# Words and stores of a float64 weight preparation moved to ScalarE, with a clamp conversion, earlier word loads and a fifth weight buffer

## The chip, the cores and the metric

One core of one Trainium2 chip. The metric is device time of the whole program in microseconds (us), the median of the runs. One run of each kernel was recorded by the profiler. Its times by stage are from that single run. The groups of experiments ran on four chips (3, 4, 5 and 14); each ratio is to the kernel before, run in the same rounds on the same chip.

## The reference

```python
# attention, per head: softmax of q over its 64 features, softmax of k over the 576 positions
q_s = exp(q - q.max(-1));  q_s = q_s / (q_s.sum(-1) + 1e-9)
k_s = exp(k - k.max(2));   k_s = k_s / (k_s.sum(2) + 1e-9)
kv  = einsum('bhsd,bhse->bhde', k_s, v)
x   = einsum('bhsd,bhde->bhse', q_s, kv)            # then heads side by side: (8, 576, 512)
# Fourier mixing, layer norm, two layers
u   = x + real(fft(fft(x, axis=1), axis=2))
un  = (u - mean(u)) / sqrt(var(u) + 1e-6)
out = u + maximum(un @ w_ch1, 0) @ w_ch2            # 512 -> 2048 -> 512; w_ch1, w_ch2 come as float64
```

## The kernel before

The two layers run as a Strassen-like scheme of 7 products. For each layer the weights are cut into 8 pairs of chunks. Each pair comes from DRAM as pairs of 32-bit words (float64), is converted, gets four additions for the seven combinations, and is stored to DRAM, from where the later batches load it. Batch 0 uses the first layer's pairs as they are prepared. The work of one batch on TensorE (PE), "up" (first layer) and "down" (second layer), is interleaved with the attention and Fourier work ("front") of the next batch.

```python
def wtile(self):                                           # the ring of weight buffers
    return self.work.tile([P, NP, HD], F32, tag="w", name="w", bufs=4)

def convert(self, place, t):                               # float64 words -> float32
    ...                                                    # lo, hi: low and high words; ti: t as int32
    nc.scalar.activation(lo, lo.bitcast(U32), ACT.Copy, scale=2.0 ** -29)
    V.tensor_scalar(out=ti, in0=hi, scalar1=3, scalar2=0x3FFFFFFF, op0=ALU.logical_shift_left, op1=ALU.bitwise_and)
    V.scalar_tensor_tensor(out=ti, in0=hi, scalar=-(1 << 30), in1=ti, op0=ALU.bitwise_and, op1=ALU.bitwise_or)
    least = float(np.array(0x38100000, np.uint32).view(np.float32))
    nc.scalar.activation(hi.bitcast(F32), hi.bitcast(F32), ACT.Abs)
    V.scalar_tensor_tensor(out=t, in0=hi.bitcast(F32), scalar=least, in1=t, op0=ALU.is_ge, op1=ALU.mult)
    nc.gpsimd.tensor_tensor(out=ti, in0=ti, in1=lo, op=ALU.add)

def prepare(self, layer, p, places):
    w = self.wtile()
    for i in range(2):
        self.convert(places[i], w[:, 2 * i:2 * i + 2, :].rearrange("p a n -> p (a n)"))
    (self.b_side if layer else self.a_side)(lambda i: w[:, i, :], nc.gpsimd, nc.vector)   # 4 additions
    if layer == 0:
        nc.sync.dma_start(self.w1s[p][:], w[:, 0:7, :]);  self.stream[p] = w
    else:
        nc.sync.dma_start(self.w2s[:, :, p, :].rearrange("s p n -> p s n"), w[:, 0:7, :])

def used(self, n):                                         # PE is done with weight tile n
    self.stream.pop(n)
    if n >= NP:
        self.load(n + 4)                                   # loads run four tiles ahead

def q_load(self, it):
    q = self.work.tile([P, D], F32, tag="q", name="q", bufs=3)
    ...
# main loop
for g in range(B + 1):
    jobs, down = blk.up(g, unT, h), blk.down(g, h)
    side = front(g + 1) ...
    cut = len(side) * 2 // 3                               # this part beside up, the rest beside down
    merged(start(blk, jobs, h) if g == 0 else flat(jobs), side[:cut])
    merged(down, side[cut:] + norm(g + 1))
```

## Time and profile before

| | before |
|---|---|
| time | 1390.59 us (1386.94 to 1391.18) |
| first product of the first layer, batch 0 | 110.2 us |
| first product of the second layer, batch 0 | 289.8 us |
| end of batch 1's first layer | 398.6 us |
| from there to the last matmul | 960.1 us |

The marks are start times of PE's instructions in the timeline. Up to the second mark PE often waits. The prediction shows the lines that this rests on.

### The profile page before, as it was taken

How to read it: one execution, taken by the hardware profiler on the slowest of the kernel's cores; microseconds unless marked ns; L12 is line 12 of the kernel's file. 1: busy time of each engine (PE TensorE's matmuls, PEld its weight loads, DVE VectorE, ACT ScalarE, POOL GpSimd, SP SyncE). 2: the span in 40 equal slices, each digit the busy share in tenths (PEclk: the TensorE clock that was granted, in tenths of full speed). 3: DMA queues.
4: the chain of work that ended last, by engine and by line, in shares of the span. 5: the costliest groups of instructions: out<-in, count | busy, mean ns of one | idle time of the engine just before them, and what ended most of it. 6: DMA issues, size and time to landing. Idle time of an engine off the chain costs nothing.

```text
span 1384.5 us, 14661 instructions
## 1 busy us (share of the span) xinstructions
PE 1226.2 (89%) x5676; PEld 1003.1 (72%) x5676; DVE 580.0 (42%) x1146; ACT 326.7 (24%) x590; POOL 422.1 (30%) x350
## 2 busy tenths in 40 slices
PE   4578677399899998999999999999999999999992
PEld 3437563288787876788778877887788778788882
DVE  3948876821513254335713542364234242502200
ACT  2624342410310142114301421142014101201200
POOL 1624566710530125003600450045013401321310
PEclk7558785589999999999999999999999999999996
DMA  5922334575342543156424542454253335455421
GB/s 170 306 68 69 137 128 163 190 265 164 141 152 88 172 159 146 67 167 198 158 98 138 193 159 77 145 197 152 88 146 130 150 103 174 150 178 179 165 102 45
DMA packets 90279, 203.46 MB, mean 147 GB/s; under 512 B 22241, under 2 KB 56033, under 8 KB 82145
## 3 DMA queue, kind: packets, MB, share of 16 engines
q1 hardware_dynamic: 90208, 202.52, 43.2%
q8 instruction: 45, 0.74, 0.2%
q14 instruction: 26, 0.20, 0.0%
HBM read 177.33 MB, written 29.88 MB: 150 GB/s over the span
## 4 chain that ended last, share of the span: by engine, by line
PE 74%; DVE 10%; POOL 6%; DMA 4%; issue 2%; ACT 1%; SPq 0%; POOLq 0%; DVEq 0%; ACTq 0%
PE bb L590 14%; PE bb L555 11%; PE bc L590 9%; PE ba L590 9%; PE ba L555 7%; PE bc L555 6%; PE acc L402 5%; DMA q<-in_q_dram 3%; PE acc L289 3%; PE acc L427 2%; POOL w L192 1%; PE acc L424 1%; PE tr L486 1%; PE acc L405 1%; POOL eo L384 1%
## 5 line engine op out<-in xcount | busy, mean ns | idle before, releaser
L555 PE MATMUL bb<-unT,w 128*128 128x256 f32 x864 | 218.8, 395 | 46.6 <-DVE u L525 39.6
L555 PEld LDWEIGHTS bb<-unT,w 128*128 128x128 f32 x864 | 166.5, 197 | 78.3 <-DVE u L525 46.3
L590 PE MATMUL bb<-w,h 128*128 128x256 f32 x864 | 198.5, 381 | 0.0
L590 PEld LDWEIGHTS bb<-w,h 128*128 128x128 f32 x864 | 161.5, 190 | 28.4 <-issue 7.3
L555 PE MATMUL ba<-unT,w 128*128 128x256 f32 x576 | 142.5, 387 | 0.0
L196 POOL TENSOR_TENSOR h<-h 128x512 f32<-128x512 f32 x36 | 46.1, 1279 | 313.4 <-ACT h L567 313.4
L555 PE MATMUL bc<-unT,w 128*128 128x256 f32 x576 | 140.5, 381 | 0.0
L590 PE MATMUL bc<-w,h 128*128 128x256 f32 x576 | 131.4, 381 | 0.0
L590 PE MATMUL ba<-w,h 128*128 128x256 f32 x576 | 128.0, 379 | 0.0
L590 PEld LDWEIGHTS bc<-w,h 128*128 128x128 f32 x576 | 107.5, 190 | 18.0 <-issue 4.4
L555 PEld LDWEIGHTS ba<-unT,w 128*128 128x128 f32 x576 | 109.2, 194 | 15.7 <-issue 1.0
L590 PEld LDWEIGHTS ba<-w,h 128*128 128x128 f32 x576 | 109.2, 190 | 15.4 <-issue 0.8
L555 PEld LDWEIGHTS bc<-unT,w 128*128 128x128 f32 x576 | 107.0, 190 | 15.3 <-DVE h L566 0.9
L567 ACT ACTIVATE h<-h 128x512 f32<-128x512 f32 x108 | 68.1, 631 | 190.8 <-DVE h L566 190.5
L604 POOL TENSOR_TENSOR x<-x,u 128x512 f32<-128x512 f32 x18 | 23.3, 1293 | 254.4 <-DVE u L528 172.2
L402 PE MATMUL acc<-ft,eo 128*128 128x289 f32 (+3 forms) x240 | 83.3, 472 | 7.5 <-POOL eo L386 7.4
L402 PEld LDWEIGHTS acc<-ft,eo 128*128 128x128 f32 (+3 forms) x240 | 39.6, 183 | 42.3 <-issue 26.0
L525 DVE TENSOR_TENSOR u<-bb,s 128x512 f32<-128x512 f32 x45 | 31.0, 689 | 89.1 <-PE bb L555 54.3
L318 POOL TENSOR_TENSOR q<-q,qm 128x512 f32<-128x512 f32 x36 | 41.8, 1170 | 82.2 <-DVE qm L317 33.1
L528 DVE TENSOR_TENSOR u<-bb,s 128x512 f32<-128x512 f32 x45 | 31.0, 689 | 77.5 <-PE bb L555 45.4
L289 PE MATMUL acc<-v,ks 128*128 128x128 f32 (+1 forms) x320 | 55.5, 317 | 6.1 <-ACT ks L277 4.1
L566 DVE TENSOR_TENSOR h<-bc,u 128x512 f32<-128x512 f32 x72 | 49.6, 689 | 24.0 <-PE bc L555 23.0
(134 smaller groups left out, 1540.0 us busy)
## 6 DMA issues: line engine op xcount, KB each, us to landing
w<-w2s SPq DMA_DIRECT2D x63, 1024.0 KB
w<-w1s SPq DMA_DIRECT2D x64, 896.0 KB
k<-in_kT_dram SPq DMA_DIRECT2D x32, 288.0 KB
h<-in_w_dram SPq DMA_DIRECT2D x18, 512.0 KB
v<-in_v_dram SPq DMA_DIRECT2D x32, 256.0 KB
q<-in_q_dram SPq DMA_DIRECT2D x32, 256.0 KB
w1s<-w SPq DMA_DIRECT2D x8, 896.0 KB
w2s<-w SPq DMA_DIRECT2D x8, 896.0 KB
```

The costliest lines, as they stand in the source:

```text
L196: e1.tensor_tensor(out=at(4), in0=at(2), in1=at(3), op=ALU.add)
L289: nc.tensor.matmul(pk, lhsT=ks[0:n, c, :], rhs=v[0:n, c, :], start=(c == 0), stop=(c == NC - 1))
L318: nc.gpsimd.tensor_tensor(out=heads, in0=heads, in1=spread(m), op=ALU.subtract)
L402: nc.tensor.matmul(pz, lhsT=eo[c][int(odds)][s, cols], rhs=self.ft[s, 3 * int(odds) + c, :], start=(c == 0), stop=(c == 2 and odds))
L427: nc.tensor.matmul(pb, lhsT=z(2 + k), rhs=self.cd[:, 2 + k, 0:HD - 1], start=(k == 0), stop=(k == 1))
L525: V.tensor_tensor(out=temp("u2"), in0=box["bb"][:], in1=box["s1"][:], op=ALU.add)
L528: V.tensor_tensor(out=temp("u3"), in0=box["bb"][:], in1=box["s1"][:], op=ALU.add)
L555: nc.tensor.matmul(bank()[:, i, :], lhsT=w[:, A_AT[m], k * P:(k + 1) * P], rhs=unT[:, B_AT[m], k, :], start=first and i == 0 and k == 0, s ...
L566: V.tensor_tensor(out=at(i), in0=bank[:], in1=u[:], op=ALU.add)
L567: nc.scalar.activation(at(i), at(i), ACT.Relu)
L590: nc.tensor.matmul(bank()[:, i, :], lhsT=h[:, p, A_AT[m], i * P:(i + 1) * P], rhs=w[:, p, :], start=first and i == 0 and p == 0, stop=p == ...
L604: nc.gpsimd.tensor_tensor(out=x, in0=x, in1=t[:], op=ALU.add)
```

## The change

The intent: the start waits on SyncE's one queue and on VectorE (DVE), whose instructions take longer beside GpSimd's (in the trace before the 32 of L185 take 0.42 us on average where no GpSimd instruction runs beside them, 16 times, and 0.91 us, up to 1.52, where one does). So words and stores go to ScalarE's (ACT's) queue, the first layer's words are asked for during batch 0's attention, all combinations go to DVE, the conversion gets a cheaper clamp, batch 0's queries get buffers of their own, and a fifth buffer lets a fifth pair be ready early. The diff, cut to its core:

```diff
-        return self.work.tile([P, NP, HD], F32, tag="w", name="w", bufs=4)
+        return self.work.tile([P, NP, HD], F32, tag="w", name="w", bufs=5)
 def words(...)
-            self.nc.sync.dma_start(place..., w1[...])
+        dma = self.nc.scalar.dma_start
 def convert(...)
+        least = float(np.array(0x38000000, np.uint32).view(np.float32))
+        nc.scalar.activation(t, hi.bitcast(F32), ACT.Abs)
+        V.tensor_scalar_max(t, t, least)
+        V.tensor_scalar(out=ti, in0=ti, scalar1=3, scalar2=0x3FFFFFFF, op0=ALU.logical_shift_left, op1=ALU.bitwise_and)
         V.scalar_tensor_tensor(out=ti, in0=hi, scalar=-(1 << 30), in1=ti, op0=ALU.bitwise_and, op1=ALU.bitwise_or)
-        V.scalar_tensor_tensor(out=t, in0=hi.bitcast(F32), scalar=least, in1=t, op0=ALU.is_ge, op1=ALU.mult)
 def prepare(...)
-        (self.b_side if layer else self.a_side)(lambda i: w[:, i, :], nc.gpsimd, nc.vector)
+        (self.b_side if layer else self.a_side)(lambda i: w[:, i, :], self.nc.vector, self.nc.vector)
+    def send(self, layer, p, w):                       # called one pair later
+        self.nc.scalar.dma_start(to, w[:, 0:7, :])
+    def follow(self, t):                               # called after each exp of batch 0's keys and queries
+        if self.first:
+            place, run = self.first.pop(0)
+            self.nc.scalar.copy(place[0:1, 0:1], t[0:1, 0:1])
+            run()                                      # issues one pair of first-layer words
 def q_load(...)
+        if b == 0:
+            q = self.halves()[:, 0:D]                  # six other buffers, not the three of "q"
 def t_load(...): three fewer loads of the shared first query
-            steps.insert(2, blk.tables)
+            steps.insert(4, blk.tables)
-        cut = len(side) * 2 // 3
+        cut = len(side) * (1 if g == 0 else 2) // 3
+            weights.early()                            # before batch 0's front
+            merged(weights.first(jobs), [])
+            merged(weights.second(), side[:cut])
```

More of the change, by code (lines that the diff above doesn't have):

```diff
@@ L137, in __init__ @@
         self.cd = c.tile([P, 5, NN], F32, name="cd")
-        self.xs, self.live, self.stream = {}, {}, {}
+        self.xs, self.live, self.stream, self.first = {}, {}, {}, []
         self.turns = 0
@@ L164, in wtile, with words, convert @@
     def wtile(self):
-        return self.work.tile([P, NP, HD], F32, tag="w", name="w", bufs=4)
-    def words(self, layer, f, place):
+        return self.work.tile([P, NP, HD], F32, tag="w", name="w", bufs=5)
+    def words(self, layer, p, place):
+        dma = self.nc.scalar.dma_start
         if layer == 0:
-            w1 = self.w1.bitcast(I32).rearrange("(k p) n -> p k n", p=P)
-            self.nc.sync.dma_start(place.bitcast(I32).rearrange("p (k n) -> p k n", k=KT),
-                                   w1[:, :, f * 2 * P:(f + 1) * 2 * P])
-        else:
-            w2 = self.w2.bitcast(I32).rearrange("(f p) n -> p f n", p=P)
-            self.nc.sync.dma_start(place.bitcast(I32), w2[:, f, :])
-    def convert(self, place, t):
+            w1 = self.w1.bitcast(I32).rearrange("(k p) (i f n) -> i p k f n", p=P, i=2, f=NP)
+            for i in range(2):
+                dma(place[:, i * 2 * D:(i + 1) * 2 * D].bitcast(I32).rearrange("p (k n) -> p k n", k=KT),
+                    w1[i, :, :, p, :])
+        else:
+            w2 = self.w2.bitcast(I32).rearrange("(i f p) n -> p i f n", p=P, i=2)
+            dma(place.bitcast(I32).rearrange("p (i n) -> p i n", i=2), w2[:, :, p, :])
+    def convert(self, place, t, adder):
         nc, V = self.nc, self.nc.vector
@@ L181, in convert @@
         ti = t.bitcast(I32)
-        nc.scalar.activation(lo, lo.bitcast(U32), ACT.Copy, scale=2.0 ** -29)
-        V.tensor_scalar(out=ti, in0=hi, scalar1=3, scalar2=0x3FFFFFFF, op0=ALU.logical_shift_left,
+        least = float(np.array(0x38000000, np.uint32).view(np.float32))
+        nc.scalar.activation(t, hi.bitcast(F32), ACT.Abs)
+        V.tensor_scalar_max(t, t, least)
+        V.tensor_scalar(out=ti, in0=ti, scalar1=3, scalar2=0x3FFFFFFF, op0=ALU.logical_shift_left,
                         op1=ALU.bitwise_and)
         V.scalar_tensor_tensor(out=ti, in0=hi, scalar=-(1 << 30), in1=ti, op0=ALU.bitwise_and, op1=ALU.bitwise_or)
-        least = float(np.array(0x38100000, np.uint32).view(np.float32))
-        nc.scalar.activation(hi.bitcast(F32), hi.bitcast(F32), ACT.Abs)
-        V.scalar_tensor_tensor(out=t, in0=hi.bitcast(F32), scalar=least, in1=t, op0=ALU.is_ge, op1=ALU.mult)
-        nc.gpsimd.tensor_tensor(out=ti, in0=ti, in1=lo, op=ALU.add)
+        nc.scalar.activation(lo, lo.bitcast(U32), ACT.Copy, scale=2.0 ** -29)
+        adder.tensor_tensor(out=ti, in0=ti, in1=lo, op=ALU.add)
     def a_side(self, at, e1, e2):
@@ L206, in b_side, with prepare @@
         e1.tensor_tensor(out=at(6), in0=at(2), in1=at(5), op=ALU.subtract)
-    def prepare(self, layer, p, places):
-        nc = self.nc
+    def prepare(self, layer, p, place):
         w = self.wtile()
         for i in range(2):
-            self.convert(places[i], w[:, 2 * i:2 * i + 2, :].rearrange("p a n -> p (a n)"))
-        (self.b_side if layer else self.a_side)(lambda i: w[:, i, :], nc.gpsimd, nc.vector)
+            self.convert(place[:, i * 2 * D:(i + 1) * 2 * D],
+                         w[:, 2 * i:2 * i + 2, :].rearrange("p a n -> p (a n)"), self.nc.gpsimd)
+        (self.b_side if layer else self.a_side)(lambda i: w[:, i, :], self.nc.vector, self.nc.vector)
         if layer == 0:
-            nc.sync.dma_start(self.w1s[p][:], w[:, 0:7, :])
             self.stream[p] = w
-        else:
-            nc.sync.dma_start(self.w2s[:, :, p, :].rearrange("s p n -> p s n"), w[:, 0:7, :])
+        return w
+    def send(self, layer, p, w):
+        to = self.w2s[:, :, p, :].rearrange("s p n -> p s n") if layer else self.w1s[p][:]
+        self.nc.scalar.dma_start(to, w[:, 0:7, :])
     def load(self, n):
@@ L268, in k_exp @@
         self.live[it].append(rec)
+        self.follow(k)
+    def follow(self, t):
[3 more added lines that the diff above has]
+            run()
     def k_turn(self, it):
@@ L296, in q_load @@
         _, b, c, u = it
-        q = self.work.tile([P, D], F32, tag="q", name="q", bufs=3)
+        if b == 0:
+            q = self.halves()[:, 0:D]
+        else:
+            q = self.work.tile([P, D], F32, tag="q", name="q", bufs=3)[:]
         for part, tok in tokens(c, u):
@@ L303, in t_load @@
         _, b, u = it
-        q = self.work.tile([P, D], F32, tag="q", name="q", bufs=3)
+        q = self.work.tile([P, D], F32, tag="q", name="q", bufs=3)[:]
+        dma = self.nc.sync.dma_start
+        if not u:
+            dma(q[0::Q], self.q[b:b + 4, 0, :])
         for j in range(4):
-            for part, tok in tokens(2, u):
-                part = slice(Q * j + part.start, Q * j + part.stop)
-                self.nc.sync.dma_start(q[part], self.q[b + j, tok, :])
+            part, tok = tokens(2, u)[-1]
+            dma(q[Q * j + part.start:Q * j + part.stop], self.q[b + j, tok, :])
         self.live[it] = [q]
@@ L313, in q_exp @@
         q = self.live[it][0]
-        heads = q[:].rearrange("p (h d) -> p h d", h=H)
+        heads = q.rearrange("p (h d) -> p h d", h=H)
         spread = lambda t: t[:].unsqueeze(2).to_broadcast([P, H, DH])
@@ L318, in q_exp @@
         nc.gpsimd.tensor_tensor(out=heads, in0=heads, in1=spread(m), op=ALU.subtract)
-        nc.scalar.activation(q[:], q[:], ACT.Exp)
+        nc.scalar.activation(q, q, ACT.Exp)
+        self.follow(q)
         rec = self.small.tile([P, H], F32, tag="qrec", name="qrec", bufs=3)
@@ L677, in flat @@
         return [s for step in steps for s in step]
-    for step in front(0):
-        step()
-    for step in norm(0):
-        step()
     for g in range(B + 1):
+        h = hpool.tile([P, NP, 7, HD], F32, tag="h", name="h")
+        if g == 0:
+            weights = Weights(blk, h)
+            weights.early()
+            merged(front(0) + norm(0), [])
         unT = nexts.pop(g)
-        h = hpool.tile([P, NP, 7, HD], F32, tag="h", name="h")
         jobs, down = blk.up(g, unT, h), blk.down(g, h)
@@ L690 @@
             side = blk.reload() if g + 1 == B else []
-        cut = len(side) * 2 // 3
+        cut = len(side) * (1 if g == 0 else 2) // 3
         if g == 0:
-            first = start(blk, jobs, h)
-            merged(first, side[:cut])
+            merged(weights.first(jobs), [])
+            merged(weights.second(), side[:cut])
         else:
@@ L698 @@
         merged(down, side[cut:] + (norm(g + 1) if g < B else []))
-def start(blk, jobs, h):
-    at = h[:].rearrange("p a s n -> p (a s n)")
-    inside = lambda r: at[:, r * 2 * D:(r + 1) * 2 * D]
-    places = {}
-    def fetch(layer, p, where):
-        places[layer, p] = where
-        for i in range(2):
-            blk.words(layer, p + i * NP, where[i])
-    def prepare(layer, p):
-        blk.prepare(layer, p, places.pop((layer, p)))
-    def fetch_in(layer, p, r):
-        return lambda: fetch(layer, p, [inside(r), inside(r + 1)])
-    def fetch_out(p, spare):
-        def run():
-            if spare:
-                t = blk.work.tile([P, 7, 2, HD], F32, tag="unT", name="words", bufs=1)[:].rearrange(
-                    "p a k n -> p (a k n)")
-            else:
-                t = blk.wtile()[:].rearrange("p a n -> p (a n)")
-            fetch(1, p, [t[:, i * 2 * D:(i + 1) * 2 * D] for i in range(2)])
-        return run
-    def ready(layer, p):
-        return lambda: prepare(layer, p)
-    steps = [fetch_in(0, p, 2 * p) for p in range(3)] + [fetch_in(0, p, 2 * p - 2) for p in range(4, NP)]
-    steps += [ready(0, 0), fetch_in(0, 3, 0)] + [ready(0, p) for p in range(1, 4)]
-    steps += jobs[0] + [ready(0, 4), ready(0, 5)] + jobs[1] + [ready(0, 6), ready(0, 7), fetch_in(1, 0, 12)]
-    steps += jobs[2] + [ready(1, 0), fetch_out(1, False), ready(1, 1)] + jobs[3]
-    for p in range(2, NP):
-        steps += [fetch_out(p, p % 2 == 0), ready(1, p)]
-    return steps + [lambda i=i: blk.load(NP + i) for i in range(4)]
@@ new lines, with __init__, fetch, ready @@
+class Weights:
+    def __init__(self, blk, h):
+        self.blk, self.h, self.places, self.last = blk, h[:].rearrange("p a s n -> p (a s n)"), {}, None
+    def fetch(self, layer, p, at):
+        def run():
+            place = self.h[:, at * 4 * D:(at + 1) * 4 * D] if isinstance(at, int) else at()[:, 0:4 * D]
+            self.blk.words(layer, p, place)
+            self.places[layer, p] = place
+        return run
+    def ready(self, layer, p):
+        def run():
+            w = self.blk.prepare(layer, p, self.places.pop((layer, p)))
+            self.send()
+            self.last = (layer, p, w)
+        return run
+    def send(self):
+        if self.last is not None:
+            self.blk.send(*self.last)
+        self.last = None
+    def early(self):
+        for p in (0, 1, 2, 4, 5, 6, 7):
+            at = p if p < 3 else p - 1
+            self.blk.first.append((self.h[:, at * 4 * D:(at + 1) * 4 * D], self.fetch(0, p, at)))
+    def first(self, jobs):
+        ready, fetch = self.ready, self.fetch
+        steps = [ready(0, 0), fetch(0, 3, 0)] + [ready(0, p) for p in range(1, 5)]
+        steps += jobs[0] + [ready(0, 5), ready(0, 6)]
+        steps += jobs[1] + [ready(0, 7), fetch(1, 0, 6), ready(1, 0)]
+        return steps + jobs[2] + [fetch(1, 1, self.ring), ready(1, 1)] + jobs[3]
+    def second(self):
+        steps = []
+        for p in range(2, NP):
+            steps += [self.fetch(1, p, self.ring if p % 2 else self.spare), self.ready(1, p)]
+        return steps + [self.send] + [lambda i=i: self.blk.load(NP + i) for i in range(4)]
+    def ring(self):
+        return self.blk.wtile()[:].rearrange("p a n -> p (a n)")
+    def spare(self):
+        return self.blk.work.tile([P, 7, 2, HD], F32, tag="unT", name="words", bufs=1)[:].rearrange("p a k n -> p (a k n)")
```

## The prediction

> **What bounds the kernel now.** I read the page first, then the busy times by stretch, then the DVE and GpSimd groups of the first 290 us, then who waited for whom in that stretch, for the queue of SyncE (SP) too. In the slices of the page PE is full from about 290 us on, and before that its clock falls to half again and again:
>
> ```profile
> PE   4578677399899998999999999999999999999992
> DVE  3948876821513254335713542364234242502200
> PEclk7558785589999999999999999999999999999996
> ```
>
> The stretches are cut at three marks of PE's timeline: 110 us (batch 0's attention, Fourier step and norm are done, the first product of the first layer starts), 204 us (the first layer of batch 0 is done), 290 us (the first product of the second layer starts). The columns are span, busy us of each engine with instruction counts, granted clock, DMA share, GB/s.
>
> ```profile
> 0.00:110.00 110.00, 61.91 (x203) 40.18 (x204) 66.13 (x143) 40.91 (x75) 39.01 (x45) 0.62 0.55 179
> 110.00:204.00 94.00, 70.14 (x341) 59.99 (x340) 77.31 (x126) 34.23 (x63) 52.27 (x43) 0.86 0.32 108
> 204.00:290.00 86.00, 52.81 (x161) 33.83 (x160) 59.30 (x113) 29.97 (x53) 50.61 (x42) 0.54 0.62 204
> 290.00:1384.50 1094.50, 1041.38 (x4977) 869.05 (x4975) 377.24 (x765) 221.60 (x401) 280.21 (x221) 0.98 0.42 143
> ```
>
> After 290 us PE is busy 1041 of 1094 us at clock 0.98, and some 26 us of what is missing is the closing tail: nothing in the change can take much there. Before 290 us PE does 185 us of work, much of it at half clock; busy times clock is 61.91 x 0.62 + 70.14 x 0.86 + 52.81 x 0.54 = 127 us, so 163 us of the start are lost. The start is where float64 weights, held as pairs of words, become float32: 8 pairs of chunks of each layer, each with two conversions, additions for the seven combinations, and a store. The second layer's product cannot start before the last of these stores has landed. So the path is: batch 0's front, conversions, first layer (its weights are kept in 4 buffers, so pairs 4 to 7 wait until PE has used pairs 0 to 3), conversions of the second layer, store, load.
>
> In this path DVE is the engine nearest to full (77.3 of 94 us, then 59.3 of 86), and much of its time isn't its own. The GpSimd row belongs to the same work (columns: busy us, mean ns):
>
> ```profile
> L191 DVE SCALAR_TENSOR_TENSOR w<-h,w 128x512 f32<-128x512 f32 x18 | 22.1, 1232 | 1.2 <-ACT h L190 1.1
> L187 DVE SCALAR_TENSOR_TENSOR w<-h,w 128x512 int32<-128x512 int32 x18 | 16.4, 914 | 0.0
> L185 DVE TENSOR_SCALAR w<-h 128x512 int32<-128x512 int32 x18 | 13.0, 735 | 0.2 <-PE bc L555 0.2
> L192 POOL TENSOR_TENSOR w<-w,h 128x512 int32<-128x512 int32 x18 | 25.9, 1444 | 26.9 <-DVE w L191 23.7 <-DVE qrec L322 2.5 <-issue 0.7
> ```
>
> The reader is to compare these means with the undisturbed durations of the same instructions, which the view of a single line gives: 0.68, 0.68, 0.42 and 1.27 us. The loss is 0.55 + 0.23 + 0.32 = 1.1 us of DVE per conversion.
>
> The second thing is order. SP issues everything, in one queue, and a store whose data isn't ready stops the loads behind it. These are SP's waits from 20 to 110 us (total, times, longest):
>
> ```profile
> SPq L216 <- DVE w L199: 39.8, 3, 24.3
> SPq L251 <- PE tr L279: 17.4, 1, 17.4
> SPq L299 <- DVE q L324: 8.7, 2, 6.3
> ```
>
> L216 is the store of combinations. In SP's timeline it stands waiting from 78 to 103 us, and only at 120.7 us is the next load of batch 1's keys issued. L299 is a load of queries that waits for one of three buffers: batch 0's query loads go out at 22.9, 33.9 and 39.5 us, and the first words of weights only at 25.4 us, though the DMA engines moved only 20 to 90 GB/s from 18 to 24 us and reach over 330 when fed.
>
> [...]L185 takes 0.42 us alone and up to 1.52 us[...]. [...]here 1.27 against 0.69 us for 128x512, so 1.84, and 0.72 against 0.42 for the 128x256 of the combinations. [...]
>
> **The change part by part.**
>
> Conversion. The clamp takes the place of the comparison and product: one tensor_scalar maximum (taken as L185's 0.42 us, same shape and kind) for the 0.685 us of L191. DVE per conversion: 0.42 + 0.42 + 0.685 = 1.53 us instead of 1.79. ACT stays at two instructions of 0.67 us.
>
> Combinations. All four additions of a pair go to DVE: 1.68 us instead of 0.84 (layer one) or 0.42 (layer two). DVE per pair, undisturbed: 2 x 1.53 + 1.68 = 4.7 us, against 4.4 and 4.0 before. GpSimd per pair: 2 x 1.27 = 2.5 us, against 4.0 and 4.7 undisturbed.
>
> Sum of both. Undisturbed DVE rises by 8 x 0.3 + 8 x 0.7 = 8 us. As run before, the conversions and combinations took DVE some 100 us (layer one 16 x 2.88 + 11.0 = 57, layer two 37.2 + 5.5 = 43), of which 33 us are over the undisturbed times. GpSimd's share in this work falls from some 83 us to about 43, so I halve the 33: DVE becomes 16 x 4.7 + 17 = 92. Only 7 us come from here; but the hops DVE to GpSimd to DVE within a pair go (POOL waited 44.8 us for L191 in all, DVE 12.7 us in the second and third stretches for GpSimd's parts of a pair).
>
> Early words. Seven of eight pairs of the first layer (1 MB each) are issued from ScalarE as keys and queries have been exponentiated, from about 6 us on, and batch 0's queries get buffers of their own. To land in the first stretch: 8.4 MB of words, 3.5 of attention inputs, 0.5 of shared queries, 1.65 of tables, 14 MB; at some 340 GB/s that is 41 us, against about 65 before. DVE sits idle for some 23 us before 35 us and 19 between 69 and 104; five pairs (the fifth buffer) fit there. The first stretch is bounded by the queries' chain, then by the Fourier step at half clock (48 us from 62 to 110, unchanged). The last queries come about 13 us earlier: 110 becomes 97.
>
> First layer. Five pairs are ready instead of four, only three are left (3 x 5.7 = 17 us of DVE with contention, instead of 28), and batch 1's attention isn't merged in as main work but fills gaps. PE needs 4 x 14 us for the four jobs; at 18 us each with the waits, 72 instead of 94: minus 22.
>
> Second layer. Six pairs at 5.7 us are 34 us, the rest of batch 1's front and norm some 20 us on DVE: 54 against 59 before, so nothing from work. Fetches no longer stand behind SP's stores (55 us of SP's waits from 110 to 290 are at the second layer's stores): 86 becomes 78.
>
> After that. Less of batch 2's front is done ahead (some 10 us of PE time at full clock lie in 266 to 290 now), partly given back by the fifth weight buffer, which lets SP issue loads without waiting for PE: plus 4.
>
> Cost on ScalarE: 16 + 8 loads of words and 16 stores, 40 issues of about 0.4 us (SP's durations) and seven tiny copies of 0.19 us, 17 us in 290, where it is busy 105; beside other work unless a send waits. Three fewer query loads per shared block save 1.5 us of SP, hidden.
>
> Sum: -13 - 22 - 8 + 4 = -39 us; 1390.6 - 39 = 1352.
>
> **The rivals.** (a) ScalarE becomes the blocked queue: a store or fetch in its order waits, and the evictions behind it stop PE. For: SP waited up to 24 us on one store. Against: each store is put one pair later, when its data should be done. It would give back 20 to 30 us: 1375 to 1385. (b) DVE is the bound and the added combinations fill what contention frees: then only the first stretch gains, 1375. (c) Early words compete with keys and queries for the same DMA engines and the front isn't shorter: the first stretch's 13 us go, 1365. (d) Freed order lets batch 1's keys come 40 us earlier and fill DVE's holes, so that the start is nearly DVE's own work (190 us at 85%, 225 us, then store and load): 1325.
>
> **Range and chances.** (a) and (b) set the upper end, 1385, (d) the lower, 1322. The 2% line is at 1363, 11 us above my number; errors of 15 to 20 us in three guessed stretches leave a good quarter above it. Faster 0.66, same 0.31, slower 0.03.
>
> **What would show each step.** The second layer's first product should start at about 247 us instead of 290; the first layer's at about 97. Mean DVE times of the conversion should fall towards 0.42 and 0.69, with GpSimd's busy time 40 us less. First words on ScalarE's queue before 10 us. SP's waits at stores of combinations gone. ACT waits for DMA or DVE at issues would show rival (a); a start at 110 us, rival (c). The prediction is wrong if the first matmul of the second layer isn't well before 275 us, or if what is gained there is lost after it.

L185 is the instruction of "The change" with 0.42 us alone and 0.91 us beside GpSimd; "here 1.27 against 0.69 us" is a two-input addition on GpSimd against one on DVE, both undisturbed and both from the trace before. That half of DVE's 33 us would go was the estimate from these times. "Over 330 when fed" is 341 GB/s, from 41 to 60 us of the trace before.

## More of the kernel before

The program text gives one order; the order in which each engine's instructions finally stand is fixed when the kernel is built, and changes with it.

## The result, and the profile after

The changed kernel takes 1429.51 us (1426.68 to 1433.51, 4 runs) against 1390.68 (1386.94 to 1391.18, 4 runs). The ratio is 1.0287, 95% interval 1.0252 to 1.0323: slower. Ratios here are the mean time of one kernel's fast runs over that of the other's in the same rounds, so they are not quite the ratio of the medians quoted.

The slices of the page after, as those of before in the prediction (each is 35.8 us long now):

```profile
PE   3477760699889989998899889988998999999992
...
DVE  1868667505351336332714261337133423412200
...
PEclk7758875699999999999999999999999999999996
```

PE no longer stays at 9 after the start: 8s recur through the steady batches, beside the deep hole at the seventh slice. To see where the 47 us of the two spans come from, both traces are cut at three marks (columns as in the prediction: span, busy us with instruction counts of PE, weight load, DVE, ACT, GpSimd; clock, DMA share, GB/s). Before:

```profile
0.00:110.00 110.00, 61.91 (x203) 40.18 (x204) 66.13 (x143) 40.91 (x75) 39.01 (x45) 0.62 0.55 179
110.00:289.80 179.80, 122.75 (x500) 93.62 (x499) 136.61 (x238) 64.20 (x115) 102.88 (x85) 0.71 0.46 154
289.80:398.60 108.80, 103.59 (x497) 90.16 (x497) 34.27 (x57) 19.47 (x34) 31.20 (x25) 1.00 0.47 158
398.60:1384.50 985.90, 937.99 (x4481) 779.09 (x4479) 342.96 (x708) 202.13 (x367) 249.01 (x196) 0.98 0.41 141
```

After:

```profile
0.00:116.00 116.00, 59.42 (x203) 38.15 (x204) 66.99 (x159) 41.22 (x82) 33.79 (x39) 0.66 0.52 170
116.00:277.90 161.90, 89.08 (x369) 71.77 (x368) 112.42 (x207) 48.85 (x90) 63.57 (x49) 0.72 0.49 170
277.90:420.90 143.00, 134.91 (x628) 111.00 (x627) 53.59 (x112) 31.34 (x57) 33.12 (x26) 0.94 0.37 128
420.90:1431.70 1010.80, 949.17 (x4481) 788.49 (x4479) 341.30 (x710) 202.67 (x368) 248.61 (x196) 0.97 0.39 136
```

Three readings:

- The second layer's first product does come 12 us earlier (277.9 against 289.8). But PE has then done 203 + 369 = 572 matmuls instead of 703. The other 131 are front work of the next batches. They are done in the third stretch, where PE is full anyway: 628 instead of 497, 31 us more of busy time. By the end of batch 1's first layer both kernels have done the same 1200, and the changed one is 22 us late. **This end is the right mark for the start**, not the second layer's first product.
- The first stretch got longer, not shorter: 116 us instead of 110.
- The last stretch has the same 4481 matmuls and takes 25 us more.

The DVE and GpSimd (POOL) rows that answer to those in the prediction, for the first 290 us (busy us, mean ns):

```profile
L192 DVE SCALAR_TENSOR_TENSOR w<-h,w 128x512 int32<-128x512 int32 x18 | 18.4, 1033 | 0.1
L188 DVE TENSOR_SCALAR w<-w 128x512 f32<-128x512 f32 x32 | 17.4, 552 | 4.9 <-ACT w L187 4.9
L195 POOL TENSOR_TENSOR w<-w,h 128x512 int32<-128x512 int32 x18 | 24.3, 1351 | 49.3 <-DVE w L192 41.5 <-issue 4.0 <-DVE krec L273 2.9
```

The clamp (L188) costs 0.55 us on average, the comparison and product 1.03 us over all 32 conversions (1.23 over the 18 that the prediction shows). All conversions together took DVE 83.0 us before and 69.5 us after, while the combinations on DVE rose from 16.5 to 35.2. The work itself is not where the time went.

Who waited for whom on PE from 200 to 280 us after:

```profile
PE acc L368 <- ACT qT L356: 34.4, 2, 33.7
```

and from 340 us to the end of PE's work:

```profile
PE tr L290 <- ACT k L271: 21.8, 6, 3.6
```

The first is a single wait of 33.7 us for the eviction of transposed queries by ScalarE. The second is up to 3.6 us long and comes six times, the first time at 373 us, still in batch 1's first layer; the kernel before has no such wait after 338 us.

### The profile page after: what moved, and what is told of

It reads as the page before. It is cut to its first block, busy times and chain, and to the rows that moved or that the text cites. A ratio compares the mean times of both kernels' runs of the same rounds, so it can differ in the third digit from the quotient of the medians.

```text
span 1431.7 us, 14667 instructions
## 1 busy us (share of the span) xinstructions
PE 1232.6 (86%) x5676; PEld 1009.4 (71%) x5676; DVE 574.3 (40%) x1186; ACT 324.1 (23%) x597; POOL 379.1 (26%) x310
## 4 chain that ended last, share of the span: by engine, by line
PE 69%; DVE 6%; POOL 3%; ACT 2%; issue 2%; DMA 1%; ACTq 0%; POOLq 0%; DVEq 0%
PE bb L610 13%; PE bb L575 10%; PE ba L610 9%; PE bc L610 9%; PE ba L575 7%; PE bc L575 6%; PE acc L422 4%; PE acc L303 3%; PE acc L447 1%; PE tr L290 1%; PE tr L506 1%; PE acc L444 1%; POOL q L337 1%; PE acc L368 1%; POOL eo L404 1%
## 5 line engine op out<-in xcount | busy, mean ns | idle before, releaser
L575 PEld LDWEIGHTS bb<-unT,w 128*128 128x128 f32 x864 | 169.9, 199 | 64.2 <-DVE u L545 26.7
L575 PE MATMUL ba<-unT,w 128*128 128x256 f32 x576 | 152.9, 405 | 2.2 <-ACT s L542 2.1
L575 PEld LDWEIGHTS ba<-unT,w 128*128 128x128 f32 x576 | 114.9, 205 | 20.8 <-ACT s L542 2.9
L624 POOL TENSOR_TENSOR x<-x,u 128x512 f32<-128x512 f32 x18 | 23.2, 1290 | 266.6 <-DVE u L548 179.4
L422 PE MATMUL acc<-ft,eo 128*128 128x289 f32 (+3 forms) x240 | 79.6, 453 | 10.1 <-POOL eo L406 8.0
L368 PE MATMUL acc<-kvr,qT 128*128 128x128 f32 x256 | 38.8, 303 | 43.6 <-ACT qT L356 36.2
L368 PEld LDWEIGHTS acc<-kvr,qT 128*128 128x128 f32 x256 | 35.2, 212 | 48.1 <-ACT qT L356 37.7
L303 PE MATMUL acc<-v,ks 128*128 128x128 f32 (+1 forms) x320 | 59.8, 334 | 10.4 <-DVE ks L294 5.0
```

Of the source, the lines that this page charges most:

```text
L303: nc.tensor.matmul(pk, lhsT=ks[0:n, c, :], rhs=v[0:n, c, :], start=(c == 0), stop=(c == NC - 1))
L368: nc.tensor.matmul(px[:, r * P:(r + 1) * P], lhsT=qT[:, r, :], rhs=self.kvr[b % 2][:, r, :], start=True, stop=True)
L422: nc.tensor.matmul(pz, lhsT=eo[c][int(odds)][s, cols], rhs=self.ft[s, 3 * int(odds) + c, :], start=(c == 0), stop=(c == 2 and odds))
L575: nc.tensor.matmul(bank()[:, i, :], lhsT=w[:, A_AT[m], k * P:(k + 1) * P], rhs=unT[:, B_AT[m], k, :], start=first and i == 0 and k == 0, s ...
L624: nc.gpsimd.tensor_tensor(out=x, in0=x, in1=t[:], op=ALU.add)
```

## The experiments

"Before" kernels were run beside each group: 1388.22, 1388.94, 1388.23, 1388.20 and 1388.47 us (7 runs each). All results were correct, and all timings had three rounds. The table gives the marks from each one's trace, so that only two columns need to be read: the **start** (end of batch 1's first layer) and the **rest** (from there to the last matmul).

| kernel | first product, layer 1 | layer 2 | start | rest | ratio to before |
|---|---|---|---|---|---|
| before | 110.2 | 289.8 | 398.6 | 960.1 | 1 |
| after | 116.2 | 277.9 | 420.9 | 985.0 | 1.0287 |
| b_w5 | 111.1 | 282.0 | 398.5 | 981.6 | 1.0121 |
| a_w4 | 111.5 | 279.9 | 413.8 | 957.6 | 1.0096 |
| a_stsp | 113.3 | 277.2 | 413.3 | 982.6 | 1.0250 |
| a_cut | 115.0 | 286.3 | 419.4 | 984.9 | 1.0304 |
| b_conv | 102.6 | 270.9 | 392.2 | 964.7 | 0.9966 |
| b_q | 100.9 | 284.4 | 394.7 | 962.3 | 0.9952 |
| a_spw4 | 115.7 | 277.2 | 399.3 | 960.4 | 0.9994 |
| a_l2spw4 | 109.5 | 272.4 | 394.0 | 960.7 | 0.9996 |
| b_both | 99.4 | 268.3 | 389.3 | 960.7 | 0.9925 |
| a_start5 | 110.7 | 259.9 | 391.2 | 963.9 | 0.9945 |
| a_l2cut | 111.0 | 274.6 | 398.9 | 958.2 | 0.9977 |
| a_late | 107.9 | 271.1 | 395.4 | 960.8 | 0.9945 |
| a_splate | 99.9 | 261.4 | 382.8 | 961.2 | 0.9874 |
| b_w5lead | 110.2 | 283.3 | 397.5 | 958.7 | 0.9980 |
| b_both5 | 99.0 | 261.1 | 374.8 | 961.1 | 0.9816 |
| a_lead5 | 115.9 | 278.3 | 412.4 | 959.0 | 1.0065 |
| a_splate5 | 98.0 | 244.3 | 374.8 | 962.3 | 0.9817 |

The rest takes only two values: some 961 us (957.6 to 964.7), or some 983 (981.6 to 985.0), the latter exactly in the four kernels with a ring of five buffers whose loads run four tiles ahead.

My theories after the result: **S**, the fifth buffer changes the steady batches for the worse (the rest); **A**, ScalarE's one queue holds its evictions behind stores and words (the start); rival to both: the front of batch 1 was only put in another place (`cut`), and rival **C**, early words get in the way of keys and queries.

### b_w5: the fifth buffer alone, in the kernel before

```diff
-        return self.work.tile([P, NP, HD], F32, tag="w", name="w", bufs=4)
+        return self.work.tile([P, NP, HD], F32, tag="w", name="w", bufs=5)
```

> The kernel before with five weight buffers instead of four, nothing else. Theory S (the fifth buffer alone gives the instructions another static order, and that order costs 7 us in each of the first layers of batches 3 to 6): those first layers take 77 to 80 us instead of 67 to 70, total 1415 to 1425 us. Rival R (the loss in these layers comes from the shared queries' loads or the ScalarE queue): 1385 to 1392 us, first layers as before.

Measured: 1405.07 us, ratio 1.0121 (1.0092 to 1.0150). One number, 4 to 5, costs some 17 us, less than the 1415 to 1425 us expected. The first layers of batches 3 to 6 take 77.1, 76.8, 77.6 and 73.1 us instead of 69.9, 70.4, 70.5 and 66.8. At the start nothing comes of it (398.5 against 398.6).

Where do 7 us per batch come from? PE's timeline of b_w5 in batch 4 (start, length, instruction, count, idle before it and what ended it):

```profile
778.45 1.89 PE L555 MATMUL bc<-unT,w 128*128 128x256 f32 x8
783.96 0.66 PE L276 MATMUL tr<-ident,k 128*128 128x128 f32 x4 [3.62 <-ACT k L265]
...
785.35 2.52 PE L289 MATMUL acc<-v,ks 128*128 128x128 f32 x10 [0.19 <-ACT ks L277]
```

and DVE's:

```profile
780.37 0.69 DVE L566 TENSOR_TENSOR h<-bc,u 128x512 f32<-128x512 f32 x1 [1.03 <-PE bc L555]
780.98 0.74 DVE L262 TENSOR_REDUCE km<-k 128x1 f32<-128x576 f32 x1
```

DVE's reduction of the third chunk of keys (L262) stands right behind an eviction (L566) that needs PE's last product. The exponential follows on ScalarE, and PE has in its own order nothing between that product and the transposes of those keys. So PE stands still for 3.62 us. It then runs slow: ten matmuls take 2.52 us, against 1.47 for the same ten elsewhere in this batch. The trace has five such waits, and the ten matmuls after each take 2.52 to 2.80 us. The granted clock of the first layers of batches 3 to 6 is 0.93 to 0.96, in the kernel before 0.98 to 1.00. The changed kernel's trace has six waits of 3.62 to 3.63 us ahead of the same transposes, and in the 4 us after each the granted clock is 0.50 to 0.69. In batch 3 the loss is 77.09 - 69.94 = 7.15 us: 2.93 us more busy time (69.43 against 66.50), the other 4.22 us waits. In the kernel before the reduction of the third keys stands ahead of those evictions, and there is no such wait.

### a_w4: the whole change without the fifth buffer

```diff
-        return self.work.tile([P, NP, HD], F32, tag="w", name="w", bufs=5)
+        return self.work.tile([P, NP, HD], F32, tag="w", name="w", bufs=4)
```

> The changed kernel with four weight buffers. Theory S: the first layers of batches 3 to 6 return to 67 to 71 us, total 1395 to 1405 us. Rival R: they stay at 73 to 80 us and the start loses some, total 1430 us or more.

Measured: 1400.87 us, ratio 1.0096 (1.0069 to 1.0124). Theory S holds: the rest is back at 957.6 us, and by the ratios 1.9 of the 2.9% lost are explained. The start is still 15 us late (413.8, of 22 us with the buffer), so the fifth buffer isn't all.

### a_stsp: the whole change with the stores on SyncE

```diff
-        self.nc.scalar.dma_start(to, w[:, 0:7, :])
+        self.nc.sync.dma_start(to, w[:, 0:7, :])
```

> The changed kernel with the stores of combinations issued by SyncE again, the words still by ScalarE. Theory A (a store waiting in ScalarE's order holds the conversions and evictions behind it): PE's wait of 34 us for the evicted queries at 212 us goes, the second layer of batch 0 starts at 262 to 270 us instead of 278, total 1405 to 1418 us. Rival (DVE or the words' landing sets the pace of the second layer's pairs): start within 4 us of 278, total 1425 to 1433 us.

Measured: 1422.69 us, ratio 1.0250 (1.0225 to 1.0275). Some 0.4% or 5 us less than the whole change, though the two intervals overlap; the start falls from 420.9 to 413.3. PE's wait of 34 us is gone, so the store was part of it. But four other waits of 7.9 to 11.6 us stand in its place (195 to 285 us), and the second layer starts at 277.2 us, as the rival had it. The words that ScalarE fetches are still in its queue.

### a_cut: two thirds of batch 1's front beside the second layer's preparation

```diff
-        cut = len(side) * (1 if g == 0 else 2) // 3
+        cut = len(side) * 2 // 3
```

> The changed kernel with two thirds of batch 1's front, instead of one third, beside the second layer's conversions. Theory C (a third is too little: what was done before 290 us in the kernel before is pushed into the second layer of batch 0 and the first of batch 1): the stretch from the second layer's start to the first layer of batch 1 shrinks from 63 to about 50 us, that first layer from 80 towards 65 us, total 1405 to 1415 us. Rival (ScalarE is blocked there anyway, so the work can't be done earlier): the start of the second layer slips by as much, total 1425 to 1433 us.

Measured: 1430.18 us, ratio 1.0304 (1.0277 to 1.0331): nothing. The second layer starts 8.4 us later (286.3), its first down is 7.5 us shorter. That the front was only put in the wrong place does not explain the loss here. a_l2cut below asks again with ScalarE's queue free.

### b_conv and b_q: two parts of the change alone, in the kernel before

b_conv takes over `convert` and puts all combinations on DVE. b_q takes over batch 0's query buffers, the merged loads and the later tables.

```diff
 b_conv: the new convert(), and
-        (self.b_side if layer else self.a_side)(lambda i: w[:, i, :], nc.gpsimd, nc.vector)
+        (self.b_side if layer else self.a_side)(lambda i: w[:, i, :], nc.vector, nc.vector)
 b_q: the new q_load() and t_load(), and
-            steps.insert(2, blk.tables)
+            steps.insert(4, blk.tables)
```

> The kernel before with only the new conversion (clamp, all four combination additions on DVE). Theory K (the conversion is sound by itself, what it saves is small: some 7 us of DVE and the hops to GpSimd): the second layer of batch 0 starts at 278 to 286 us instead of 290, total 1376 to 1387 us. Rival (the additions on DVE cost what contention frees): start at 288 to 294 us, total 1388 to 1395 us.

> The kernel before with only the new query loads (own buffers for batch 0's queries, one load for the shared token of four batches, tables two steps later). My prediction's step (queries some 13 us earlier, the first layer starts earlier): first layer at 97 to 104 us, total 1378 to 1386 us. Rival (the front is bounded by the Fourier step and DVE, or the order changes against it): first layer at 107 to 114 us, total 1386 to 1396 us.

Measured: b_conv 1383.64 us, ratio 0.9966 (0.9950 to 0.9982); b_q 1381.55, ratio 0.9952 (0.9933 to 0.9971). Both are gains, and both small. In b_conv the second layer starts 18.9 us earlier (270.9), but the start is only 6.4 us shorter: 662 matmuls are done by then instead of 703, and the first layer of batch 1 takes 71.1 us instead of 60.4. In b_q the first layer starts at 100.9 us instead of 110.2.

### a_l2spw4 and a_spw4: ScalarE's queue freed

Both have four buffers and all stores on SyncE. In a_l2spw4 the second layer's words go to SyncE too; in a_spw4 all words do.

```diff
-        dma = self.nc.scalar.dma_start
+        dma = self.nc.sync.dma_start if layer else self.nc.scalar.dma_start     # a_l2spw4
+        dma = self.nc.sync.dma_start                                            # a_spw4
```

> The changed kernel with four weight buffers, the first layer's words issued by ScalarE as in the change, the second layer's words and all stores by SyncE. Theory A: the harm is in the stretch where ScalarE must also evict for PE, so this is as good as issuing all from SyncE or better: 1372 to 1390 us. Rival (the early words themselves crowd out keys and queries): 5 us or more slower than with SyncE alone, since both have the early words only if the gate on SyncE works too, so within 3 us of it would speak for the queue as the cause.

> The changed kernel with four weight buffers and every weight transfer issued by SyncE again. With the fifth buffer out of the way, theory A (ScalarE's order is what keeps PE waiting 33 us for evicted queries near 212 us): that wait goes and the 10 to 13 us that the four-buffer version is slower than the kernel before are gone: total 1375 to 1390 us. Rival (they come from the clamp, the queries or the smaller share of batch 1's front): total 1397 to 1405 us, with PE still idle for 30 us in one piece.

Measured: a_l2spw4 1385.97 us, ratio 0.9996 (0.9966 to 1.0027); a_spw4 1386.73, ratio 0.9994 (0.9968 to 1.0021). Against a_w4 the start of a_l2spw4 falls from 413.8 to 394.0 us: theory A holds, with 20 us. How it looks on ScalarE in the changed kernel (ACTq lines are DMA issues):

```profile
221.41 0.66 ACT L194 ACTIVATE words<-words 128x512 int32<-128x512 uint32 x1
226.68 0.37 ACTq L225 DMA_DIRECT2D w2s<-w  x1
227.15 0.52 ACTq L177 DMA_DIRECT2D w<-in_w_dram  x1
233.58 0.37 ACTq L225 DMA_DIRECT2D w2s<-w  x1
234.80 0.66 ACT L187 ACTIVATE w<-w 128x512 f32<-128x512 f32 x1 [12.73 <-DMA w<-in_w_dram]
...
245.28 0.59 ACT L356 COPY qT<-tr 128x512 f32<-128x512 f32 x1
```

From 222.1 us ScalarE has nothing to compute. Its store waits 4.6 us for DVE's last addition, which ends at 226.60 us; only then can the next words be asked for, and the next conversion waits for them to land. The eviction of the queries, transposed by PE by 212 us, stands behind all this in program order and comes at 245.28 us. That is the 33.7 us of PE. So in this trace ScalarE's evictions and its DMA issues went in one order: what PE had ready by 212 us was copied at 245.28 us, after the issues ahead of it. In a_l2spw4 PE's wait for L356 is 2.1 us; a wait for DVE of 21.9 us has become the longest from 200 to 280 us:

```profile
PE tr L352 <- DVE q L344: 21.9, 1, 21.9
...
PE acc L368 <- ACT qT L356: 2.1, 2, 1.7
```

### b_both: conversion and query loads together, in the kernel before

The edits of b_conv and b_q in one kernel.

> The kernel before with the new conversion and the new query loads together; words and stores stay on SyncE, four weight buffers, two thirds of batch 1's front beside the second layer. Alone they gave -5.3 and -7.4 us. If the two parts take different waits (conversion the second layer's preparation, queries the first stretch) they add up: some 1377 us, first product of the first layer at 97 to 100 us, of the second layer at 268. If both only move the start while PE's work ahead of time is lost by the same amount, nothing more comes: 1382 us.

Measured: 1377.54 us, ratio 0.9925 (0.9894 to 0.9955). Within the noise the two gains add up (0.34% + 0.48% against 0.75%), which fits parts that take different waits.

### a_start5: a fifth buffer for the start only

a_l2spw4, with one more buffer that holds pair 4 of the first layer once and isn't in the ring.

```diff
-        w = self.wtile()
+        w = self.wtile() if (layer, p) != (0, 4) else self.work.tile([P, NP, HD], F32, tag="w5", name="w5", bufs=1)
```

> The changed kernel with second layer's words and all stores on SyncE and four ring buffers, plus a fifth weight buffer that holds only pair 4 of the first layer and is never used again. If the loss of the fifth buffer lies in the order of the steady batches, and not in the buffer as such, then the first layers of batches 3 to 6 stay at 66 to 72 us, and the first layer of batch 0 is some 5 us shorter: 1381 to 1386 us. If a fifth buffer in itself harms[...], the first layers go back to 73 to 80 us and the time is near 1410.

Measured: 1382.43 us, ratio 0.9945 (0.9920 to 0.9969). The rest stays at 963.9 us: a fifth buffer as such does no harm.

### a_l2cut: the front's place again

a_l2spw4 with the edit of a_cut.

> The same kernel (second layer's words and all stores on SyncE, four buffers) with two thirds of batch 1's front beside the second layer's preparation instead of one third. In the kernel with the whole change this moved work without gain (start of the second layer +8.4 us, first down -7.5). If the front fits in PE's waits once ScalarE's queue is free, the first down shrinks by 3 us and the first layer of batch 1 by up to 8 without the start slipping: 1378. If DVE is what fills the preparation, the start slips as much as the rest gains: 1386.

Measured: 1385.26 us, ratio 0.9977 (0.9954 to 1.0001). Undecided within a few us; if anything, the start is later (398.9).

### a_late: a failed test of the early words

a_l2spw4, with the words issued after batch 0's front in program order.

```diff
-            weights.early()
...
+        steps = [fetch(0, p, p if p < 3 else p - 1) for p in (0, 1, 2, 4, 5, 6, 7)]
```

> The same kernel (second layer's words and all stores on SyncE, four buffers), with the early words of the first layer taken away: they are issued from ScalarE after batch 0's attention, as the kernel before did from SyncE. If early words compete with keys and queries (rival c), the first product of the first layer comes earlier than 109.5 us, at some 100, and the time is 1376 to 1383. If early words are what the start gains from, the first layer of batch 0 gets longer by 10 us or more and the time is 1392 or more.

Measured: 1380.81 us, ratio 0.9945 (0.9924 to 0.9966). The run does not test what it was to test: on ScalarE's queue nothing stands before the words, and they were issued from 0.74 us on, about as early as in a_l2spw4 (nine of the loads by 27 us, there eight). Its result counts neither way.

### a_splate: the early words taken away

a_spw4 with the edit of a_late. All words now stand on SyncE behind the queries.

> The changed kernel with four weight buffers, all words and stores on SyncE, and no early words: SyncE issues the words of the first layer after batch 0's last queries, as in the kernel before. It differs from the run with early words on SyncE (first product of the first layer at 115.7 us, 1386.7 us) only in that order. If early words compete with keys and queries, the first product comes at 98 to 103 us, as in the runs of the kernel before with the change's conversion or its query loads, and the time is 1374 to 1380. If they do not, it stays at 110 to 116 and the time at 1384 to 1388.

Measured: 1371.38 us, ratio 0.9874 (0.9845 to 0.9903), against 0.9994 of a_spw4. Early words do make the front later: the first product comes at 99.9 us without them instead of 115.7. SyncE's timeline in a_splate and then in a_spw4:

```profile
17.63 2.88 SPq L327 DMA_DIRECT2D q<-in_q_dram  x7
20.56 9.12 SPq L316 DMA_DIRECT2D eo<-in_q_dram  x4
29.72 22.84 SPq L173 DMA_DIRECT2D h<-in_w_dram  x16
```

```profile
47.32 4.18 SPq L173 DMA_DIRECT2D h<-in_w_dram  x2
51.54 0.98 SPq L316 DMA_DIRECT2D eo<-in_q_dram  x2
55.63 0.38 SPq L173 DMA_DIRECT2D h<-in_w_dram  x1
56.06 0.51 SPq L316 DMA_DIRECT2D eo<-in_q_dram  x1
```

Batch 0's last queries (L316, into eo) are issued by 29.7 us in one and by 56.6 us in the other. In a_spw4 the cause is SyncE's own order: by its waits of the first 60 us it stood 23.2 us at words that had to wait for their copies, with the queries behind them. So this pair does not show a contest for the DMA engines, as rival C has it. Nearer to the change is a_l2spw4, with the early words on ScalarE: against it a_splate's first product comes 9.6 us earlier (109.5 to 99.9) and its start is 11.2 us shorter (394.0 to 382.8).

In the changed kernel itself, with words on ScalarE, the last queries are issued from 34.54 to 39.50 us. There the keys suffer as well: the fourth chunk, asked for at 18.74 us, is reduced on DVE at 27.77 us, where DVE had waited for it; in the kernel before that is at 18.66 us. SyncE's waits there, from 0 to 60 us, name the words:

```profile
SPq L257 <- DMA h<-in_w_dram: 6.0, 1, 6.0
SPq L261 <- DMA h<-in_w_dram: 3.9, 2, 2.3
SPq L327 <- DMA h<-in_w_dram: 3.8, 2, 3.4
...
SPq L260 <- DMA h<-in_w_dram: 2.5, 1, 2.5
```

By this view loads of keys, values and queries stood 16.2 us unissued until words had landed; a_splate has no such wait. The DMA engines were also busier: 0.87 of the first 34 us, at 270 GB/s, against 0.60 and 190 in a_splate. Rival C's effect is shown; how much of it is the shared DMA engines and how much the held issues, no run separates.

### b_w5lead: five buffers, five tiles ahead

b_w5, with the loads put one tile further ahead.

```diff
-            self.load(n + 4)
+            self.load(n + 5)
-    return steps + [lambda i=i: blk.load(NP + i) for i in range(4)]
+    return steps + [lambda i=i: blk.load(NP + i) for i in range(5)]
```

> The kernel before with five weight buffers and weights loaded five tiles ahead instead of four, so that each load again has to wait for a buffer that PE has just left, as with four buffers. With five buffers and four ahead it took 1405 us, first layers of batches 3 to 6 at 77.1, 76.8, 77.6, 73.1. If the loss is only that the load no longer waits for PE and so is placed ahead of the next batch's keys in SyncE's order, the first layers go back to 70 us and the time to some 1380 (8 us gained at the start). If any change of depth gives a worse order of instructions in the steady batches, they stay above 73 and the time near 1400.

Measured: 1386.82 us, ratio 0.9980 (0.9953 to 1.0006). The first layers of batches 3 to 6 are at 71.6, 70.9, 70.9 and 69.9 us: the loss is gone, as expected. **But the reason that I gave for it isn't the one.** In SyncE's timeline the weights still stand ahead of the next keys: in batch 4 the third load of keys is issued at 788.07 us, 43 us after the batch's first product (in b_w5 44 us after it, in the kernel before 24 us). What differs is PE's order:

```profile
771.46 1.89 PE L555 MATMUL bc<-unT,w 128*128 128x256 f32 x8
773.19 1.03 PE L555 MATMUL ba<-unT,w 128*128 128x256 f32 x4
774.05 1.03 PE L555 MATMUL bb<-unT,w 128*128 128x256 f32 x4
774.91 1.03 PE L555 MATMUL bc<-unT,w 128*128 128x256 f32 x4
776.98 0.66 PE L276 MATMUL tr<-ident,k 128*128 128x128 f32 x4 [1.04 <-ACT k L265]
```

DVE's reduction stands behind the same eviction as in b_w5, but PE has twelve matmuls of the next products (2.6 us) between the product and the transposes. The wait is 1.04 us instead of 3.62, and no slow clock follows: after each of the five such waits of this trace the ten matmuls take 1.57 us, and the granted clock of the first layers of batches 3 to 6 is 1.00. By these traces the loss is where one instruction stands in PE's order relative to DVE's, and not the buffer or its loads in themselves; no run changed that order alone.

### b_both5: the best version made from the kernel before

b_both with the edit of a_start5.

> The kernel before with the new conversion, the new query loads and a fifth weight buffer that only pair 4 of the first layer uses. In the changed kernel on SyncE that buffer gave 3.5 us. If the fifth pair ready ahead shortens the first layer of batch 0 here too, 1373 us; if the start is bound by the second layer's chain of conversion, store and load, 1377 as without it.

Measured: 1363.16 us (1361.30 to 1366.05), ratio 0.9816 (0.9789 to 0.9843). This beats both kernels. I had expected at best 1373; the fifth pair is worth more here than in a_start5 (start 389.3 to 374.8).

### a_lead5: the whole change, with its fifth buffer and loads five ahead

The edit of b_w5lead in the changed kernel.

> The whole change with its five weight buffers, the weights loaded five tiles ahead instead of four. In the kernel before this took the loss of the steady batches away (1405 to 1387 us). If the same holds here, the first layers of batches 3 to 6 fall from 73-80 to 67-72 us and the time from 1429.5 to some 1402, what removing the fifth buffer gave; the wait of some 33 us at the eviction of the transposed queries stays. If ScalarE's queue was part of that loss, it falls by less than 20 us.

Measured: 1397.75 us, ratio 1.0065 (1.0042 to 1.0087). PE's wait of 33.7 us for L356 is still there, and the rest is 959.0. Five buffers can stay.

### a_splate5: all three mended

a_splate with the edit of a_start5.

> The changed kernel with all words and stores on SyncE, the words behind batch 0's queries, and the fifth weight buffer used for pair 4 only. If the three orders (early words, ScalarE's queue, fifth buffer in the ring) are the whole loss, it comes to the best kernel made from the one before, 1363 us, or some 5 us under 1371.4 at the least. If it stays at 1371, the fifth pair gains nothing here and something else of the change holds the start.

Measured: 1362.57 us (1361.98 to 1364.86), ratio 0.9817 (0.9797 to 0.9837), the same as b_both5. The three orders account for the whole loss. Its second layer starts at 244.3 us, 17 us earlier than in b_both5, and both end batch 1's first layer at 374.8 us: once more the earlier mark says nothing.

## Why the prediction was wrong

The predicted sum was -39 us, the measured one +39 in the medians (+47 in the two profiled spans). By its own steps:

- **First stretch, "110 becomes 97": wrong, +6.** Rival (c) was true in its effect, and I gave it only the loss of the gain. Batch 0's query buffers alone bring 100.9 us (b_q). From 99.9 us in a_splate to the changed kernel's 116.2, early words on ScalarE add 9.6 us (a_l2spw4, 109.5), ScalarE's stores and later words 2.0 (a_w4, 111.5), the fifth buffer 4.7. Nor did the words come "from about 6 us on": half had no gate (each pair's words are two loads, and the copy in `follow` touches the place of the first load alone). My sum "14 MB at some 340 GB/s" asked when all bytes have landed. The path asked when keys and queries land, and these lost their place.
- **First layer, -22: measured -10** (94 to 84.4 us).
- **Second layer's preparation, -8: the size was right by luck, the reason wrong.** It went from 86 to 77.5 us, but PE left 131 matmuls of front work undone by then. Rival (a) was true here: "each store is put one pair later, when its data should be done" failed, as the store still waited for DVE, and the next words stood behind it. It cost 20 us of the start (a_w4 against a_l2spw4), the 20 to 30 I had put on it, yet I left it out of the sum.
- **"After that", +4: the step that failed most, measured +59.** 34 us of it lie between the second layer's first product and the end of batch 1's first layer (108.8 to 143.0 us): some 25 are the work not done ahead, as a_w4 with the same 628 matmuls takes 133.9, and some 9 the fifth buffer. I saw that work ("some 10 us of PE time") but counted a third of it, and put first among my signs the second layer's first product, which it doesn't touch. At 277.9 us that was not "well before 275", and what was gained there was lost after it. 25 us are the steady batches. There I had the fifth buffer "give back" time; alone it costs 17 us in the kernel before (b_w5).
- **DVE and GpSimd: GpSimd's share right, DVE's not.** GpSimd's busy time fell by 43 us, predicted 40. DVE's conversions and combinations: 99.5 us before (predicted "some 100"), then 104.7 where 92 was predicted. I had halved the 33 us over the undisturbed times to 17; 29.5 stayed (104.7 less 75.2): the additions took 35.2 us, not the undisturbed 27, the conversions 69.5, not 49. Still the conversion is a gain by itself, 0.34% (b_conv).
- **Two readings that don't hold as written**, though the sum doesn't rest on them: the loss of 1.1 us per conversion is that of the 18 conversions shown, over all 32 it is 0.8 (means 1.03, 0.92 and 0.65 us); and the DMA engines moved 118 GB/s from 20 to 22 us (64 from 18 to 24), so not "20 to 90" throughout.

The loss, added up in ratios from the change back to its mended form: fifth buffer in the ring -1.9% (a_w4), ScalarE's queue -1.0% (a_l2spw4), early words -1.2% (a_splate against a_spw4 or a_l2spw4, which agree), and a further -0.6% for the fifth pair at the start (a_splate5).

What stays open: why the fifth pair is worth 14 us at the start in b_both5, 8 in a_splate5 and 3 in a_start5; what a_late's 5 us are; and in what way early words hold up the keys and queries. Nor is it shown that the slow clock comes from the idle time. It follows all eleven waits of 3.6 us in b_w5 and the changed kernel, and none of the five of 1.04 us in b_w5lead. But the length of a wait alone doesn't decide: in the kernel before, the granted clock of the next 4 us is 1.00 after a wait of 3.33 us (to 366.4 us) and 0.64 after one of 2.08 us (to 510.7 us). No run varies the idle time alone.

## What to carry to other kernels

ScalarE's queue was one order here: a DMA issue that waited for data held the eviction behind it, and PE lost 33.7 us in one piece. With the second layer's words and all stores on SyncE the start was 20 us shorter (a_w4, a_l2spw4). So before a store or a fetch is given to an engine, look for what PE needs behind it there. Words asked for ahead of the path's own keys and queries were no gain: the first product came at 115.7 us with them and at 99.9 without (a_spw4, a_splate). One more buffer in the ring changed the order of instructions and cost 17 us (b_w5): look at the steady stage after such an edit, and judge a start by a mark at which both kernels have done the same number of matmuls.
